# A gated mix of two attentions on one core: small vector work moved to GpSimd and ScalarE, and more score tasks and all projection jobs run before the attention loop

## The chip, the core and the metric

The kernel runs on one core of a Trainium2 chip. Its engines work side by side, each with a queue of its own in program order: TensorE (PE, with its weight loads as PEld), VectorE (DVE), ScalarE (ACT), GpSimd (POOL), and SyncE (SP), which issues most DMA transfers. The metric is the device time of one execution in microseconds; the median over several executions counts.

## The reference

Two attentions over the same input `x` (2048 × 512, 32 heads of 16) are mixed by a gate per row. A is causal within four segments of 512 rows, with a linear memory carried from segment to segment; B is full attention over all 2048 rows.

```python
def _A_ref(x, wq, wk, wv, wo, beta):            # H = 32; Dh = 16; N = 4 segments; L = 512
    ...
    phi = lambda t: jnp.where(t > 0, t + 1.0, jnp.exp(t))
    for s in range(N):
        qs, ks, vs = q[:, :, s], k[:, :, s], v[:, :, s]
        p = _softmax(jnp.einsum("bhqd,bhkd->bhqk", qs, ks) * scale + mask, axis=-1)
        a_dot = jnp.einsum("bhqk,bhkd->bhqd", p, vs)
        pq = phi(qs)
        num = jnp.einsum("bhld,bhde->bhle", pq, M)
        den = jnp.einsum("bhld,bhd->bhl", pq, z)[..., None] + 1e-6
        outs.append(g * num / den + (1.0 - g) * a_dot)
        pk = phi(ks)
        M = M + jnp.einsum("bhld,bhle->bhde", pk, vs)
        z = z + jnp.einsum("bhld->bhd", pk)
    return o @ wo
def _B_ref(x, wqkv, wo):
    ...
    p = _softmax(jnp.einsum("bhqd,bhkd->bhqk", q, k) * (Dh ** -0.5), axis=-1)
    o = jnp.einsum("bhqk,bhkd->bhqd", p, v)
    return o.transpose(0, 2, 1, 3).reshape(B, S, D) @ wo

g = _sigmoid((x * gate_w).sum(-1, keepdims=True))
return g * a + (1 - g) * b
```

## The kernel before

The work falls into two stages.

**The projection stage** computes V, Q and K of both attentions. Operands are split in a high and a low part, so that one job is three products: 12 matmuls into one PSUM bank (`v_job`, `qk_job`), then a rounding on ACT (line 348) and the remainder on DVE (line 349), and a store to DRAM by SP. After V of A and the first group of B, a loop over 16 blocks (`blk`) takes the Q and K of A, block by block of 128 columns by 512 rows, with the memory's updates between. Into its gaps two kinds of work are put: **fill jobs**, the 40 remaining jobs of B, in the order of the list `fill`, as many by the end of each block as `CUM` says; and **score tasks**, by `spill()`, two at a time whenever `quota` has grown to 2. 38 of these tasks (`first`) belong to the first units of both attentions, and the first `EARLY` tasks of unit 33 (`early`) come behind them. Four fill jobs are left over for slot 0.

**The attention loop** has 32 **slots**. Slot `k` handles unit `32 + k` of B and unit `k` of A; a unit is four heads by 512 query rows. In a slot PE makes 32 steps of B and 5 of A. A step (`t_group`) makes two score blocks, transposed so that keys lie on partitions, into two of three PSUM banks (line 635); ACT takes their exponentials into SBUF (line 641); for A, POOL zeroes what the causal mask excludes (line 644); and PE multiplies with V (`pv`, line 657), two steps later, into one bank, `PVB`, that all of it shares. `fin_copy` copies that bank out when a unit is complete: for B at the slot's end on ACT (line 666), for A at the start of the next slot on DVE (line 664).

The softmax's row maxima have to be known ahead. So the scores of unit `33 + k` of B and of `k + 1` of A are computed once more in slots before, in **score tasks** (`s_b`, line 572; `s_a`, line 550), 32 and 6 per slot, each with one maximum on DVE over 128 × 1024 (lines 574, 558, 560). Two PSUM buffers, `SBK`, hold them. `m_chain(k + 1)` gathers the maxima in step pair 10 of a slot (line 583), scales them and splits them in two fp16 parts (lines 597 to 599 on DVE, or 592 to 595 on POOL), and `m_rows` transposes them on PE and sends them into rows of the query tile, where the score matmul subtracts them.

`beside(k, it)` places the rest by step pair `it`: `fin_load` reads a finished unit back in another layout; `fin_rec` takes reciprocals of the denominators on DVE and multiplies them by the gates (line 687 or 689 on DVE; 684, 685, 689 on POOL); `fin_bc` spreads them over 64 partitions by DMA into `d`; `fin_norm` multiplies (line 701, POOL), every second slot. The output weights are read in slots 1 to 4 by `load_wo`, which also splits them (lines 713 and 714, POOL). From slot 9 on, the output projection (`out_rows`) is part of the slots.

The order on every engine is the order in which the program issues instructions; nothing reorders it, apart from the semaphores' waits.

Of the kernel before, what the change touches and what calls it, by code (L numbers as in the profile page):

```python
# [28 lines left out]
FAR = 2.0 ** 15  # L29
TOP = 2.0  # L30
WIDE = 2.0 ** 13
EARLY = 6
S_FIRST = 10
S_LAST = 10
OMI = 14
SPILLS = 64


@with_exitstack
def gated_mix_kernel(ctx, tc, xt, wq, wk, wv, wo, beta, wqkv, wob, gate_w, out):  # L40
    nc = tc.nc
# [536 lines left out]
    def m_chain(k):  # L578
        mx = pair_max(k)
        if k == 1:  # L580
            nc.vector.memset(mx[:, 0], 0.0)
        if k < 32:
            nc.vector.tensor_reduce(mx[:, 1], MXB.pop(32 + k).rearrange("q j p i c -> q (j p) i c"), axis=AX.X,
                                    op=OP.max)
        else:
            nc.vector.memset(mx[:, 1], 0.0)
        del MX[k]
        mx = mx.rearrange("q u h i -> q (u h i)")
        m8 = M8[k] = W.tile([128, 2, 32], FT, name="m8")
        hi = W.tile([128, 32], HF, name="mhi")  # L590
        if 8 <= k < 32:
            nc.gpsimd.tensor_scalar(mx, mx, -1.0 / AUX, None, op0=OP.mult)
            nc.gpsimd.tensor_copy(hi, mx)
            nc.gpsimd.tensor_copy(m8[:, 0], hi)
            nc.gpsimd.tensor_tensor(m8[:, 1], mx, hi, op=OP.subtract)
        else:
            nc.vector.tensor_scalar(hi, mx, -1.0 / AUX, None, op0=OP.mult)
            nc.vector.tensor_copy(m8[:, 0], hi)
            nc.vector.scalar_tensor_tensor(m8[:, 1], mx, -1.0 / AUX, hi, op0=OP.mult, op1=OP.subtract)
# [16 lines left out]
    AT = {}  # L616
# [43 lines left out]
    def fin_copy(u):  # L660

        ps = W.tile([128, C], FT, name="pvs", bufs=1)
        if u < 31:
            nc.vector.tensor_copy(ps, PVB)
        else:
            nc.scalar.activation(ps, PVB, AF.Copy)  # L666
        AT["pd", u] = D.tile([4, 32, C], FT, name=f"pd{u}")
        nc.sync.dma_start(AT["pd", u].rearrange("h r t -> (h r) t"), ps)
# [9 lines left out]
    def fin_rec(u):  # L678
        kd, qd, c = UN[u]
        r = AT.pop(("r", u))  # L680
        nc.vector.reciprocal(r, r)  # L681
        early = u % 32 < 7 or u in (31, 63)
        if kd == "A" and not early:
            nc.gpsimd.tensor_scalar(r, r, nq[:, qd:qd + 1], None, op0=OP.mult)
            nc.gpsimd.tensor_tensor(r, r, grow[:, 0, c], op=OP.mult)
        elif kd == "A":
            nc.vector.scalar_tensor_tensor(r, r, nq[:, qd:qd + 1], grow[:, 0, c], op0=OP.mult, op1=OP.mult)
        else:
            (nc.vector if early else nc.gpsimd).tensor_tensor(r, r, grow[:, 1, c], op=OP.mult)  # L689
        AT["rd", u] = D.tile([128, E], FT, name=f"rd{u}")  # L690
        nc.sync.dma_start(AT["rd", u], r)
# [16 lines left out]

    def load_wo(g):
        for a, w in enumerate((wo, wob)):  # L710
            raw = AT["o"][1][:, g, a]
            nc.sync.dma_start(raw, w[g * 128:(g + 1) * 128, :])
            nc.gpsimd.tensor_copy(AT["wh"][:, g, a], raw)
            nc.gpsimd.tensor_tensor(AT["wl"][:, g, a], raw, AT["wh"][:, g, a], op=OP.subtract)

# [82 lines left out]
    ST_A = [(0, None), (2, 0), (2, 1), (3, 0), (3, 1), (1, None)]  # L798
# [113 lines left out]
    def spill():  # L912
        nonlocal quota
        quota += rate
        if quota >= 2:
            quota -= 2
            for _ in range(2):
                (first or early).pop(0)()

    S0 = [b[:, 0] for b in SBK]  # L920
    CUM = (2, 4, 6, 9, 11, 13, 16, 18, 20, 22, 24, 27, 29, 32, 34, 36)
    for blk in range(16):
        g, c = divmod(blk, 4)
        pg, pc = divmod(blk - 1, 4)
        if blk == 4:
            mode["misc"] = TB + [MB, PVB]
        rate = len(ST_A + ST_B) / SPILLS if 4 <= blk < 14 else 0
        if blk == 14:
            for p in range(2):
                set_aux(KB[1][:, p], 0, nc.sync)  # L930
            load_kb(1, 0)
        n = blk + 1 + (c == 2)
        if c < 3 and n < 16:
            load_vm(n // 4, n % 4)
        qk_job(0, "A", g, 0, c)
        if c == 3 and g < 3:
            split_w(0, "A", g + 1, (0,))
        spill()
        if blk == 0:
            do_beta()  # L940
        if blk == 2:
            load_kb(0)
# [24 lines left out]
        if blk == 15:  # L967
            m_rows(0)
        want = CUM[blk]
        mt = [[], [], []]  # L970
        if c > 0:
            mt[0] += [todo(mem_out, g, c)]
            mt[2] += [todo(mem_put, g, c)]
        if c < NC4 - 1:
            mt[1 + (c == 0)] += [todo(mem_tr, g, c)]
        for n in range(3):
            for f in mt[n]:
                f()
            if blk == 14 and n == 2:
                quota = EARLY  # L980
            if mt[n]:
                spill()
            if g < 3 and (c, n) == (1, 2):
                top(("A", g + 1))
            if g < 3 and (c, n) == (2, 0):
                w_rng("A", g + 1)
            if g < 3 and (c, n) == (2, 2):
                w_esc("A", g + 1)
            if blk == 14:
                load_kb(1, 1 + n)  # L990
            if nf == 35:
                mode["misc"] = [MB, PVB, TB[1]]
            if nf < want:
                fill[nf]()
                spill()
                if nf in (15, 20):
                    load_w("B", 2 + nf // 20)
                if nf in (15, 20, 26):
                    split_w(2 if nf == 20 else 1, "B", nf // 5 - 2)
                for f, at in ((w_abs, (11, 17, 22)), (lambda *a: top(a), (12, 18, 23)), (w_rng, (13, 19, 24)),  # L1000
                              (w_esc, (14, 21, 25))):
                    if nf in at:
                        f("B", at.index(nf) + 1)
                nf += 1
        if blk == 13:
            for f in first:
                f()
            first, quota = [], 0
        if 0 < c < NC4 - 1:
            mem_upd(g, c)  # L1010
        if blk == 14:
            spill()
        if blk == 15:
            for f in early:
                f()
        if nf >= 16 and "vb" not in AT:
            AT["vb"] = 1
            load_vb(0)
# [42 lines left out]
    def extras(k):  # L1061

        pre, post = {}, {}
        if not k:
            for n in range(4):
                pre[2 * n] = [fill[n - 4]]
        post[2 * S_LAST + 4] = [todo(m_rows, k + 1)]
        for n, at in [(k - 9, 1)] + [(23, 2 * OMI)] * (k == 31):
            if n >= 0:
                rows = (n // 8, n // 2 % 4, n % 2)  # L1070
                pre[at] = [todo(out_rows, *rows, plan.pop((k, at))) if k < 31 else todo(out_mm, *rows)]
        return pre, post
# [41 lines left out]
    for k in range(31):  # L1114
        if k:
            spread([todo(s_b, 33 + k, *t) for t in (sorted(ST_B, key=lambda t: t[2]) if k == 1 else ST_B)],
                   [(k - 1, n) for n in range(2 * S_FIRST, 2 * NT)] + [(k, n) for n in range(2 * S_LAST)])
        else:
            spread(st33[EARLY:], sorted([(0, n) for n in range(2 * S_LAST)] + [(0, 2 * n) for n in range(4)]))
        for n, t in enumerate(ST_A):  # L1120
            plan.setdefault((k, 2 * NT + n - (n > 2)), []).append(todo(s_a, k + 1, *t))

    ex = [extras(k) for k in range(32)]
    for k in range(32):
        ua, ub = k, 32 + k
        banks = T3 + [b[:, 0] for b in SBK] * (k == 31)
        for n in range(NG):
# [27 lines left out]
            if it == 9:  # L1155
                if k % 2 == 0 and k < 30:
                    load_vb(k // 2 + 1)
                if 1 <= k <= 4:
                    load_wo(k - 1)
    pv(31, 2)  # L1160
    fin_copy(31)
    fin_bc(63)
# [52 lines left out]
```

## Time and profile before

| | |
|---|---|
| median of 3 runs | 1825.24 us (1824.66 to 1825.6) |
| the profiled execution | 1825.88 us, of which 1824.2 are the span of the profile |
| busy: PE, DVE, ACT, POOL | 98%, 87%, 80%, 19% of the span |
| projection stage | up to 324.86 us |
| slot 0 | 324.86 us to about 389.6 us |
| slots 1 to 8, copy to copy of `fin_copy` | 45.90, 45.07, 45.47, 44.81, 44.80, 44.80, 44.28, 43.66 us |
| slots 9 to 12 | 45.73, 45.66, 45.80, 45.66 us |
| granted clock of PE | 0.996 over the span |

A line of a timeline has start, duration, engine, line of the kernel, operation, what it writes from what it reads, shapes, and in brackets the idle time of the engine ahead of it with what ended that. Matmuls overlap, so a busy PE isn't PE at its peak. The granted clock is the share of full clock that the throttle allowed PE. The shares of busy time are means over stages with different limits; a stage is read by itself.

### The profile page before, as it was taken

What the parts mean: (1) busy time and instruction counts of PE and PEld (TensorE: products, weight loads), DVE (VectorE), ACT (ScalarE), POOL (GpSimd) and SP (SyncE); (2) the same over time, 40 slices, a digit from 0 to 9 for tenths busy, and PEclk for the clock granted to TensorE, in tenths of its full rate; (3) what the DMA queues carried; (4) which work ended last, traced back from release to release, by engine and by line L of the source; (5) the groups of instructions that cost most, each with busy time, mean ns of one, the idle gap of its engine ahead of it and who ended that gap; (6) DMA issues with size and microseconds to landing.
All of it is one profiled execution on the core that took longest, in us unless ns stands there. A gap on an engine that the chain in (4) does not pass through costs nothing.

```text
span 1824.2 us, 44323 instructions
## 1 busy us (share of the span) xinstructions
PE 1786.8 (98%) x17781; PEld 645.1 (35%) x17781; DVE 1590.9 (87%) x1787; ACT 1459.3 (80%) x2741; POOL 339.5 (19%) x691
## 2 busy tenths in 40 slices
PE   8999999999999999999999999999999999999998
PEld 6554445222222222333333333333333333333325
DVE  7745786699999999999999999999999999999932
ACT  4454444588989999989898989898989898989894
POOL 4400000001212111112121222122212221222122
PEclk9999999999999999999999999999999999999999
DMA  5654534322323232223232323232323232323111
GB/s 196 152 153 134 159 104 115 75 81 73 93 74 93 64 85 70 77 65 88 65 87 67 86 70 82 71 88 69 85 69 86 68 86 68 86 66 87 46 38 62
DMA packets 162482, 158.92 MB, mean 87 GB/s; under 512 B 40140, under 2 KB 126620, under 8 KB 162276
## 3 DMA queue, kind: packets, MB, share of 16 engines
q1 hardware_dynamic: 158692, 149.29, 29.5%
q0 software_dynamic: 3296, 6.27, 1.8%
q8 instruction: 140, 2.29, 0.5%
q14 instruction: 66, 0.54, 0.1%
q10 hardware_dynamic: 288, 0.52, 0.1%
HBM read 103.38 MB, written 50.86 MB: 85 GB/s over the span
## 4 chain that ended last, share of the span: by engine, by line
PE 78%; DVE 14%; ACT 4%; issue 2%; DMA 1%; POOL 0%; SPq 0%; ACTq 0%; DVEq 0%; POOLq 0%
PE pvb L657 28%; DVE mxb L574 12%; PE tb L635 12%; PE sbk L572 9%; PE mb L635 6%; PE tb L332 3%; ACT raw L641 3%; PE tb L742 2%; PE mb L332 2%; PE sbk L550 2%; PE tb L302 2%; PE sbk L302 2%; PE pvb L332 2%; PE mb L742 1%; PE sbk L332 1%
## 5 line engine op out<-in xcount | busy, mean ns | idle before, releaser
L574 DVE TENSOR_REDUCE mxb<-sbk 128x2 f32<-128x1024 f32 x1024 | 1172.5, 1212 | 21.7 <-PE sbk L572 11.1
L641 ACT ACTIVATE raw<-tb 128x512 f32<-128x512 f32 x1555 | 884.0, 600 | 61.1 <-PE tb L635 25.1
L657 PE MATMUL pvb<-raw,vb 128*17 128x256 f32 (+1 forms) x8072 | 644.4, 388 | 0.0
L572 PE MATMUL sbk<-kb,qb 64*128 64x512 f16 x2048 | 552.7, 378 | 8.4 <-DVE mxb L574 7.3
L641 ACT ACTIVATE raw<-mb 128x512 f32<-128x512 f32 x782 | 469.1, 600 | 33.7 <-PE mb L635 16.7
L635 PE MATMUL tb<-qb,kb 64*128 64x512 f16 x1342 | 467.9, 380 | 2.4 <-ACT raw L641 1.3
L635 PEld LDWEIGHTS <-kb 64*128 64x128 f16 x2048 | 143.5, 93 | 414.1 <-issue 408.8
L657 PEld LDWEIGHTS pvb<-raw,vb 128*17 128x17 f32 x8072 | 137.8, 95 | 402.9 <-issue 393.5
L635 PE MATMUL mb<-qb,kb 64*128 64x512 f16 x679 | 258.4, 381 | 0.0
L644 POOL TENSOR_SCALAR_AFFINE_SELECT raw<-raw 128x256 f32<-128x256 f32 (+1 forms) x320 | 115.4, 361 | 324.4 <-ACT raw L641 316.0
L572 PEld LDWEIGHTS <-qb 64*128 64x128 f16 x2048 | 137.4, 93 | 44.3 <-issue 33.7
L558 DVE TENSOR_REDUCE mx<-sbk 128x2 f32<-128x1024 f32 (+1 forms) x128 | 133.9, 1088 | 6.9 <-PE sbk L554 5.7
L657 PE MATMUL pvb<-raw,va 128*17 128x256 f32 (+2 forms) x1280 | 103.2, 383 | 3.7 <-ACT pvs L666 0.9
L701 POOL TENSOR_TENSOR o<-o,d 128x512 f32<-128x512 f32 x31 | 39.5, 1273 | 217.6 <-DMA d<-rd 156.6
L560 DVE TENSOR_REDUCE mx<-sbk 128x4 f32<-128x512 f32 x64 | 60.6, 947 | 12.5 <-PE sbk L554 12.5
L550 PE MATMUL sbk<-ka,qa 64*128 64x512 f16 (+3 forms) x512 | 70.7, 296 | 0.0
L635 PE MATMUL tb<-qa,ka 64*128 64x512 f16 (+3 forms) x339 | 61.8, 302 | 0.0
L347 DVE SCALAR_TENSOR_TENSOR phi<-phe,phi 128x512 f32<-128x512 f32 x24 | 16.6, 692 | 51.6 <-ACT phe L346 51.6
L689 POOL TENSOR_TENSOR rec<-rec,grow 128x16 f32<-128x16 f32 x24 | 5.3, 222 | 275.8 <-DVE rec L681 275.8
L554 PE MATMUL sbk<-cmask,crows 64*128 64x64 bf16 x1024 | 52.7, 189 | 0.0
L332 PEld LDWEIGHTS <-ws 128*128 128x128 f16 x384 | 37.1, 98 | 43.5 <-issue 2.9
L554 PEld LDWEIGHTS <-crows 64*128 64x128 bf16 x1024 | 46.4, 94 | 13.9
(358 smaller groups left out, 1621.8 us busy)
## 6 DMA issues: line engine op xcount, KB each, us to landing
vb<-vdB SPq DMA_DIRECT2D x16, 1088.0 KB
pd<-pvs SPq DMA_DIRECT2D x64, 256.0 KB
kb<-dB SPq DMA_DIRECT2D x60, 256.0 KB
dB<-st SPq DMA_DIRECT2D x64, 128.0 KB
dA<-st SPq DMA_DIRECT2D x64, 128.0 KB
o<-pd SPq DMA_DIRECT2D x64, 128.0 KB
d<-rd SPq DMA_DIRECT2D x63, 128.0 KB
kb<-dB SPq DMA_DIRECT2D x60, 128.0 KB
```

The lines of the kernel that those rows point to most:

```text
L302: nc.tensor.matmul(b, x[:, n % 4, tl * 128:(tl + 1) * 128], (WVA if kd == "A" else WV)[wi][:, n % 4, :], start=n == 0, stop=n == 11)
L332: nc.tensor.matmul(b, WS[ws][w][wi][:, k, :], (XH, XL)[xi][c][:, k, :], start=n == 0, stop=n == 11)
L550: nc.tensor.matmul(b[:, j, c0:c0 + n], q_of(u)[r, p, i * 128:(i + 1) * 128], k_of(u, p)[r, :n], start=True, stop=False)
L554: nc.tensor.matmul(b[:, j, c0 + n - 128 + w.start:c0 + n - 128 + w.stop], crows[r, n2 - 1], cmask[r, n2 - 1, w], start=False, stop=n2 == 2)
L558: nc.vector.tensor_reduce(m[:, :, p, i], b[:, :, :n], axis=AX.X, op=OP.max)
L560: nc.vector.tensor_reduce(m[:, :, :, i], b.rearrange("q j (p k) -> q j p k", p=2)[:, :, :, :n], axis=AX.X, op=OP.max)
L572: nc.tensor.matmul(b[:, j], q_of(u)[r, p, i * 128:(i + 1) * 128], k_of(u, p)[r, kc * C:(kc + 1) * C], start=True, stop=True)
L574: nc.vector.tensor_reduce(MXB[u][:, :, p, i, kc], b, axis=AX.X, op=OP.max)
L635: nc.tensor.matmul(bs[j][:, c0:c0 + w], k_of(u, h // 2)[r, 128 * it:128 * it + 128], q_of(u)[r, h // 2, q0:], start=True, stop=True)
L641: nc.scalar.activation(pt, bs[j], AF.Exp, scale=AT["esc", kd, qd // 2])
L644: nc.gpsimd.affine_select(out=m, in_=m, pattern=[[1, 128]] if n < 2 else [[0, 2], [1, 128]], compare_op=OP.is_ge, fill=0.0, base=0, channe ...
L657: nc.tensor.matmul(PVB[32 * h:32 * h + E + 1, q0 + lo:q0 + hi], vt[:, it, 4 * q + h, :], pt[:, lo:hi], start=it == 0 and lo == 0, stop=it ...
```

## The change

Four pieces of work change engine or place.

1. `m_chain` splits the maxima on POOL for `k` from 2 on (from 8 before): that is done in slots 1 to 6 in addition. `fin_rec` multiplies the gates on POOL for all units but 0, 31, 32 and 63 (before, the units 0 to 6 and 32 to 38 had DVE).
2. `fin_copy` of A's units 0 to 7, at the starts of slots 1 to 8, moves from DVE to ACT.
3. `load_wo` only loads; `split_wo`, new, splits the output weights in step pair 14 of slots 1 to 4, and not in step pair 9.
4. `EARLY` goes from 6 to 14, `spill` starts at block 3 with 0.62 of a task per call (block 4, 0.59 before), and `CUM` ends at 40: all fill jobs and 14 tasks of unit 33 run in the projection stage; slot 0 has no fill job and 8 score tasks fewer. Unit 33's keys are loaded whole in block 7.

```diff
-EARLY = 6
+EARLY = 14
-SPILLS = 64
+RATE = 0.62
...
-        if 8 <= k < 32:
+        if 2 <= k < 32:
             nc.gpsimd.tensor_scalar(mx, mx, -1.0 / AUX, None, op0=OP.mult)
...
     def fin_copy(u):
-        if u < 31:
+        if 8 <= u < 31:
             nc.vector.tensor_copy(ps, PVB)
         else:
             nc.scalar.activation(ps, PVB, AF.Copy)
...
     def fin_rec(u):
-        early = u % 32 < 7 or u in (31, 63)
+        early = u % 32 < 1 or u in (31, 63)
...
     def load_wo(g):
         for a, w in enumerate((wo, wob)):
+            nc.sync.dma_start(AT["o"][1][:, g, a], w[g * 128:(g + 1) * 128, :])
+
+    def split_wo(g):
+        for a in range(2):
             raw = AT["o"][1][:, g, a]
-            nc.sync.dma_start(raw, w[g * 128:(g + 1) * 128, :])
             nc.gpsimd.tensor_copy(AT["wh"][:, g, a], raw)
             nc.gpsimd.tensor_tensor(AT["wl"][:, g, a], raw, AT["wh"][:, g, a], op=OP.subtract)
...
-    CUM = (2, 4, 6, 9, 11, 13, 16, 18, 20, 22, 24, 27, 29, 32, 34, 36)
+    CUM = (2, 5, 7, 10, 12, 15, 17, 20, 22, 25, 27, 30, 32, 35, 37, 40)
...
-        rate = len(ST_A + ST_B) / SPILLS if 4 <= blk < 14 else 0
-        if blk == 14:
+        rate = RATE if blk > 2 else 0
+        if blk == 7:
             for p in range(2):
                 set_aux(KB[1][:, p], 0, nc.sync)
-            load_kb(1, 0)
+            load_kb(1)
...
-            if blk == 14 and n == 2:
-                quota = EARLY
...
-            if nf == 35:
+            if nf == 39:
                 mode["misc"] = [MB, PVB, TB[1]]
...
-        if not k:
-            for n in range(4):
-                pre[2 * n] = [fill[n - 4]]
...
-            spread(st33[EARLY:], sorted([(0, n) for n in range(2 * S_LAST)] + [(0, 2 * n) for n in range(4)]))
+            spread(st33[EARLY:], [(0, n) for n in range(2 * S_LAST)])
...
                 if 1 <= k <= 4:
                     load_wo(k - 1)
+            if it == 14 and 1 <= k <= 4:
+                split_wo(k - 1)
```

What stands in POOL's queue in slot 2 before, between the masks of slot 1 and its own (the `wh` and `wl` rows are the weights' parts, `d1` and `d0` the spread denominators of B and A, `raw8` the exponentials that are masked):

```order
L701 TENSOR_TENSOR o0_2997<-o0_2997,d1_3002 128x512
L713 CAST wh_2999<-o1_2998 128x512
L714 TENSOR_TENSOR wl_3000<-o1_2998,wh_2999 128x512
...
L701 TENSOR_TENSOR o0_2997<-o0_2997,d0_3001 128x512
L644 AFFINE_SELECT raw8_86<-raw8_86 128x128 x4
L644 AFFINE_SELECT raw8_86<-raw8_86 128x2x128 x6
```

And now, in slot 2:

```order
L689 TENSOR_TENSOR rec_3911<-rec_3911,grow_82 128x16
L684 TENSOR_SCALAR rec_3987<-rec_3987,nq_85 128x16
L685 TENSOR_TENSOR rec_3987<-rec_3987,grow_82 128x16
L701 TENSOR_TENSOR o0_2991<-o0_2991,d1_2996 128x512
L592 TENSOR_SCALAR mx_3818<-mx_3818 128x32
...
L595 TENSOR_TENSOR m8_4211<-mx_3818,mhi_4212 128x32
L701 TENSOR_TENSOR o0_2991<-o0_2991,d0_2995 128x512
L716 CAST wh_2993<-o1_2992 128x512
L717 TENSOR_TENSOR wl_2994<-o1_2992,wh_2993 128x512
...
L644 AFFINE_SELECT raw8_86<-raw8_86 128x128 x4
L644 AFFINE_SELECT raw8_86<-raw8_86 128x2x128 x6
```

Gate products and the maxima's split are new to the queue, and the weights' split (twice cast and subtract) has moved from ahead of the second line-701 product to between it and the masks. Slot 4 has the same order; slots 1 and 3 have no line-701 product.

On ACT the end of the projection and the start of slot 0 stand so before (line 348 rounds a fill job, line 1106 loads the exponentials' scales into registers, line 641 is an exponential):

```order
L452 ACTIVATE om<-tb_135,gh 128x512
L1106 TENSOR_LOAD esc x8
L641 ACTIVATE raw_86<-tb_134 128x512
L641 ACTIVATE raw_86<-mb 128x512
L348 ACTIVATE st<-tb_135,xr 128x512
```

And now:

```order
L452 ACTIVATE om<-pvb,gh 128x512
L348 ACTIVATE st<-tb_135,xr 128x512
L1103 TENSOR_LOAD esc x8
L641 ACTIVATE raw_86<-tb_134 128x512
L641 ACTIVATE raw_86<-mb 128x512
L641 ACTIVATE raw_86<-tb_135 128x512
```

The last fill job's rounding has moved from behind the first two exponentials to ahead of the register loads, and no further one stands among the exponentials.

More of the change, by code (lines that the diff above doesn't have):

```diff
@@ L916, in spill @@
             quota -= 2
-            for _ in range(2):
-                (first or early).pop(0)()
+            for f in (first or early)[:2]:
+                f()
+            del (first or early)[:2]
     S0 = [b[:, 0] for b in SBK]
-    CUM = (2, 4, 6, 9, 11, 13, 16, 18, 20, 22, 24, 27, 29, 32, 34, 36)
+    CUM = (2, 5, 7, 10, 12, 15, 17, 20, 22, 25, 27, 30, 32, 35, 37, 40)
     for blk in range(16):
@@ L988, in gated_mix_kernel @@
                 w_esc("A", g + 1)
-            if blk == 14:
-                load_kb(1, 1 + n)
-            if nf == 35:
+            if nf == 39:
                 mode["misc"] = [MB, PVB, TB[1]]
```

## The prediction

> **What bounds the kernel now.** I read first the busy time by stage, cut at each copy of the P·V accumulator (line 664), since that copy is made once per slot. Columns: window, length, busy of PE, PEld, DVE, ACT, POOL, granted clock, DMA.
>
> ```profile
> 324.86:391.35 66.49, 61.28 (x562) 18.61 (x562) 54.45 (x56) 45.98 (x85) 3.61 (x10) 0.95 0.28 78
> 391.35:437.25 45.90, 44.45 (x493) 12.99 (x492) 45.17 (x49) 40.67 (x77) 7.31 (x14) 1.00 0.28 77
> 572.60:617.40 44.80, 44.25 (x493) 12.96 (x492) 44.12 (x49) 40.80 (x77) 3.61 (x10) 1.00 0.24 63
> 662.20:706.48 44.28, 44.05 (x493) 12.97 (x492) 43.66 (x46) 40.70 (x77) 4.55 (x14) 1.00 0.23 63
> 706.48:750.14 43.66, 43.45 (x492) 12.90 (x492) 43.12 (x43) 41.29 (x78) 8.93 (x20) 1.00 0.33 88
> 750.14:795.87 45.73, 45.56 (x518) 14.68 (x520) 43.90 (x45) 40.66 (x78) 6.58 (x18) 1.00 0.23 59
> ```
>
> The first row is slot 0 from its first line-635 matmul, and runs 1.8 us into slot 1. The others are slots 1, 5, 7, 8 and 9. In slots 1 to 7 DVE is filled to 0.7 us of the slot, and the slot shortens whenever DVE loses work: 44.80 to 44.28 where the maxima's split goes to POOL, to 43.66 where the gate products follow. So VectorE paces slots 1 to 8. From slot 9 on, with the output projection, DVE idles 1.83 us and PE paces; those slots are untouched by the change.
>
> The timeline of DVE in slot 1, and of PE, POOL and DVE in slots 2 and 8, show what the moved work costs where it is:
>
> ```profile
> 391.35 0.68 DVE L664 COPY pvs<-pvb 128x512 f32<-128x512 f32 x1
> 391.94 12.52 DVE L574 TENSOR_REDUCE mxb<-sbk 128x2 f32<-128x1024 f32 x11
> 415.64 0.61 POOL L713 CAST wh<-o 128x512 fp32r<-128x512 f32 x1 [25.94 <-DVE mxb L574]
> 416.74 0.91 DVE L597 TENSOR_SCALAR mhi<-mx 128x32 f16<-128x32 f32 x1
> ...
> 462.64 0.18 DVE L597 TENSOR_SCALAR mhi<-mx 128x32 f16<-128x32 f32 x1
> 463.05 11.40 DVE L574 TENSOR_REDUCE mxb<-sbk 128x2 f32<-128x1024 f32 x10
> 463.85 0.61 POOL L713 CAST wh<-o 128x512 fp32r<-128x512 f32 x1 [6.91 <-DMA o<-in_A_wo_dram]
> 465.60 0.39 PE L635 MATMUL mb<-qb,kb 64*128 64x512 f16 x1
> 466.45 1.27 POOL L714 TENSOR_TENSOR wl<-o,wh 128x512 fp32r<-128x512 f32 x1
> 472.04 1.27 POOL L701 TENSOR_TENSOR o<-o,d 128x512 f32<-128x512 f32 x1 [4.33 <-DMA d<-rd]
> 472.18 0.39 PE L635 MATMUL mb<-qb,kb 64*128 64x512 f16 x1
> 473.32 0.39 PE L635 MATMUL tb<-qa,ka 64*128 64x512 f16 x1
> 474.60 0.29 POOL L644 TENSOR_SCALAR_AFFINE_SELECT raw<-raw 128x128 f32<-128x128 f32 x1 [1.28 <-ACT raw L641]
> 476.34 0.29 POOL L644 TENSOR_SCALAR_AFFINE_SELECT raw<-raw 128x128 f32<-128x128 f32 x1 [0.20 <-ACT raw L641]
> 476.91 0.62 PE L657 MATMUL pvb<-raw,va 128*17 128x256 f32 x8
> 480.54 0.39 PE L635 MATMUL mb<-qb,kb 64*128 64x512 f16 x1
> ...
> 731.33 0.29 POOL L592 TENSOR_SCALAR mx<-mx 128x32 f32<-128x32 f32 x1 [5.12 <-DVE mx L583]
> 732.13 0.24 POOL L595 TENSOR_TENSOR m<-mx,mhi 128x32 f32<-128x32 f32 x1
> ```
>
> DVE's maximum over one score task recurs every 1.14 us (11.40 for 10). PE, where it doesn't wait, makes a step in 1.10 us (465.60 to 472.18, six steps) and the five steps of attention A in 7.2 (473.32 to 480.54). A slot therefore needs 32 × 1.10 + 7.2 + 0.3 for the rows of maxima = 42.7 us of PE. That floor is 1 us under slot 8.
>
> **The cost, part by part. Slots 1 to 8.** Their sum, copy to copy, is 750.14 − 391.35 = 358.8 us.
> - The copy goes to ACT in slots 1 to 8 (units 0 to 7). DVE gets its next maximum 0.59 us earlier each time (391.35 to 391.94). ACT has 41.3 of 43.66 us filled in slot 8, and the copy is about 0.6 there too. It stands in ACT's queue ahead of the exponentials of the second group, whose bank PE wants for the third group, and so makes PE some 0.5 later there; but DVE, a whole maximum in arrears, takes that up, so I count it as hidden. If it isn't, it costs up to 0.6 × 8 = 4.8; it can't gain beyond DVE's 0.59.
> - Splitting the maxima on POOL in slots 1 to 6, and the gate products in slots 2 to 7, brings them to what slots 7 and 8 show. On POOL the split ends at 732.37, 1.04 us after its start, and slot 8 hides that. Slot 1 keeps its products on DVE: 0.5 more there.
> - The first step of the maxima's split takes DVE 0.91 us in slot 1, where the weight split runs beside it, against 0.18 in slot 2. Moved apart, that goes too; it is part of slot 1's 45.90.
>
> So the slots go to 43.66 − 0.6 = 43.06, just over PE's floor: 8 × 43.06 + 0.5 = 345.0.
> - Against it stands the weight split's new place. In slots 1 and 3 the queue of POOL is empty behind the maxima, and nothing waits. In slots 2 and 4 the split now stands behind line 701's second product, which waits for its denominators until 472.04, and ahead of the causal masks of line 644. The split takes 3.9 us (463.85 to 467.72), so the first mask starts at 472.04 + 1.4 + 3.9 = 477.3, not 474.60. The four masks then run back to back in 1.4 and end at 478.7, not 476.63. PE's P·V at 476.91 starts 0.3 behind the last mask already, so PE waits 2 us more, and in-order behind it wait the remaining groups and their score tasks. Cost 2 × 2.0 = 4.1. The lower end is 0, if the denominators land 2.7 us earlier; the upper end is the split's whole 3.9 in both slots, 7.8.
>
> Slots 1 to 8: 349.1, a gain of 9.7 us.
>
> **Projection and slot 0.** Rows of the chain, and PE at the start of slot 0:
>
> ```profile
> 264.07 5.18 PE tb L332 x24
> 306.94 0.61 PE L572 MATMUL sbk<-kb,qb 64*128 64x512 f16 x4
> 307.48 0.73 PE L473 MATMUL tb<-vm,pk 128*128 128x136 f32 x4
> L1106 ACTq TENSOR_LOAD <-esc x8: 272/332/1269, 325.0 to 329.0; - x8
> 324.86 0.39 PE L635 MATMUL tb<-qb,kb 64*128 64x512 f16 x1
> 329.33 0.60 ACT L641 ACTIVATE raw<-tb 128x512 f32<-128x512 f32 x1 [3.49 <-PE tb L332]
> 329.98 0.37 PE L635 MATMUL tb<-qb,kb 64*128 64x512 f16 x1 [1.34 <-ACT raw L641]
> ```
>
> Four fill jobs (12 matmuls, 2.6 us) and eight score tasks (0.27 each: two take 307.48 − 306.94) enter the projection: 10.4 + 2.2 = 12.6 us of PE. Their DVE work, some 12 us, lies beside it: of the 213 us before slot 0, DVE is idle in 76. PE's waits for the rounding of a projection on DVE (line 349), behind a pair of maxima, I leave as they are:
>
> ```profile
> PE tb L302 <- DVE st L349: 1.8, 2, 1.1
> PE tb L332 <- DVE st L349: 1.4, 2, 1.0
> PE mb L332 <- DVE st L349: 1.0, 1, 1.0
> 112.00:324.86 212.86, 206.75 (x1135) 106.41 (x1135) 136.42 (x248) 92.78 (x182) 15.89 (x26) 1.00 0.48 136
> ```
>
> They sum to 4.2 us (columns: total, times, longest; the last row is the stage's busy time); I allow ±3 for the new places. Slot 0 then starts at 324.9 + 12.6 = 337.5. Unit 33's keys, loaded whole in block 7 and not in pieces from block 14, and the fills' last stores, which leave SP's queue ahead of slot 0, cost nothing: SP isn't in the chain there, and unit 33's tasks still come last of all; were the keys late, PE's score tasks would wait for them one by one.
>
> Slot 0 itself loses the fills and the DVE excess. PE needs 42.7, less the last P·V of a slot before (0.6) and two score tasks (0.5): 41.6. To this comes the start. ACT loads eight scale registers from 325.0 on, and its first exponential comes 4.5 us after PE's first score group. PE gets that bank back 5.1 us after the first matmul (329.98). The new order wants it for the second half of the second group, which a running slot reaches after one step and a matmul, some 1.3 us: 3.8 us, which a fill job filled before and nothing fills now. And the clock:
>
> ```profile
> 307.99:311.40 3.41, 2.08 (x14) 1.09 (x14) 3.41 (x5) 0.00 (x0) 0.45 (x1) 1.00 0.49 142
> 328.47:331.88 3.41, 1.08 (x7) 0.36 (x8) 0.85 (x2) 2.55 (x5) 0.00 (x0) 0.98 0.18 65
> 331.88:338.40 6.52, 6.39 (x17) 1.84 (x17) 3.35 (x3) 1.29 (x3) 0.00 (x0) 0.50 0.16 43
> ```
>
> After 3.4 us in which PE was busy for 1.1, the granted clock was 0.50 for 6.5 us; after 2.1 busy it stayed full. The new start leaves PE about 1.1 us busy in 4.5, so I take the same 6.5 us at half clock: 3.0 lost. The Trainium skill, "TensorE: Matmul & The Clock Gate", HAM oscillation, asks only for no PE-idle gap over about 3.4 us. The trace differs: the clock fell with PE's longest single gap before it at 1.34.
>
> Slot 0 to the same mark: 41.6 + 3.8 + 3.0 + 1.8 = 50.2, against 66.5. Projection and slot 0 together: 12.6 − 16.3 = −3.7.
>
> **Sum.** −9.7 − 3.7 = −13.4. The profiled execution took 1825.88 us (span 1824.2 and 1.7 around it), 0.64 above the median of 1825.24; the sum gives 1812.5 for it and 1811.8 for the median.
>
> A rule that speaks against moving work to POOL: the Trainium skill, "GPSIMD Engine Reference", Engine selection, gives elementwise work to VectorE, GpSimd being about 2x slower for two-input operations. The trace agrees on the size (1.04 us for the split on POOL; 462.64 to 463.05, 0.41, on DVE). By that rule slots 1 to 6 would lose 0.6 each, 3.8 in all, where the rows of maxima are awaited; slot 8 is shorter with the split on POOL, so they aren't.
>
> **Rivals.**
> - *PE, not DVE, paces slot 8.* Then 43.66 is the end, and the copy gains nothing: 4.8 more, 1816.6. For it: PE busy is 43.45 of 43.66. Against: steps of 1.13 there beside 1.10 unhindered. 0.16.
> - *The clock stays up at slot 0.* For it: the second group's first half breaks PE's wait in two. Against: so did the matmuls at 329.98. 3.0 less: 1808.8. 0.14. By the Trainium skill's clock page, quoted above, this is the case that comes, as neither part of the wait reaches 3.4 us.
> - *The masks aren't held up*, since faster slots bring the denominators earlier in relation: 4.1 less, 1807.7. 0.12.
> - *The 2 us waits in slots 2 and 4 drop the clock as well*: 1.4 busy of 3.4 lies nearer to the 1.1 that dropped it than to the 2.1 that didn't, but only where the clock's window falls just there. 6.5 us at half clock twice: 6.5 more, 1818.3. 0.09.
> - *Slower: the projection stage turns bank-bound.* All 26 pairs of tasks now run there, two maxima each ahead of the rounding that frees PE's bank. Were every pair to stall PE by the longest seen, 1.07, that is 27.8 instead of 4.2, and 23.6 on the sum: 1835.4. It decides from (13.4 + 4.2) / 26 = 0.68 us a pair. Against: five such waits now, with 22 pairs. 0.04.
>
> **How the numbers follow.** The forecast, 1811.8, has 0.45. The range 1804 to 1819 takes in the two faster and the two slower rivals, with ±3 for the projection's waits at its lower end, and leaves out the bank-bound case and joint extremes. A change of 0.2% is 3.65 us, about what a measurement here can tell from none: faster means below 1821.6. All cases but the last are; with 1 in 50 for mishaps among them: 0.94 faster, 0.03 the same, 0.03 slower.
>
> **What would show it.** Slots 3, 5, 6, 7, 8 at 43.0 to 43.2 copy to copy and slot 1 at 43.6; DVE idle some 1 us in each; slots 2 and 4 at about 45, with PE waiting 2 us for line 644 behind the second weight split. First line-635 matmul near 337.5, slot 0 near 48 us with half clock in its first 10. Wrong if the slots stay at 43.6 or above, or if PE's waits for line 349 in the projection exceed 9 us.

## The result, and the profile after

The changed kernel took 1817.0 us (median of 5 runs, 1816.1 to 1818.0) beside 1825.3 us of the kernel before on the same chip: a ratio of 0.9948, 95% interval 0.9935 to 0.9962. The forecast was 1811.8, its range 1804 to 1819. The profiled execution took 1818.03 us (span 1816.3), 7.9 less than that of before; the sum of the prediction had said 13.4 less. So the sign and most of the gain came, and 5.5 us of it didn't.

Busy time by stage, in the columns used before (window, length, PE, PEld, DVE, ACT, POOL, granted clock, DMA): the projection from 112 us on, slot 0 from its first line-635 matmul to the copy, then slots 1, 2, 5, 8 and 9 from copy to copy. The copies of slots 0 to 7 are ACT's now (line 666), that of slot 8 is DVE's again.

```profile
112.00:341.39 229.39, 220.35 (x1199) 111.21 (x1197) 148.89 (x260) 96.27 (x186) 15.90 (x26) 1.00 0.49 131
341.39:391.60 50.21, 45.83 (x497) 12.39 (x497) 42.70 (x44) 41.71 (x79) 3.61 (x10) 0.93 0.30 82
391.60:435.47 43.87, 43.41 (x496) 12.45 (x493) 43.16 (x44) 40.61 (x78) 8.19 (x18) 1.00 0.29 77
435.47:480.12 44.65, 43.65 (x496) 12.76 (x493) 42.80 (x42) 40.57 (x78) 11.22 (x23) 1.00 0.39 101
568.22:611.47 43.25, 42.94 (x496) 12.48 (x493) 42.62 (x42) 40.57 (x79) 5.30 (x17) 1.00 0.21 57
697.97:741.61 43.64, 43.21 (x496) 12.55 (x494) 43.01 (x42) 41.70 (x80) 8.94 (x20) 1.00 0.33 89
741.61:787.35 45.74, 45.58 (x518) 14.68 (x520) 43.91 (x44) 40.66 (x78) 6.58 (x18) 1.00 0.21 57
```

Four readings, each against a row of before:
- Slots 1 to 8 last 741.61 − 391.60 = 350.0 us, not 358.8: −8.8. All but slots 2 and 4 (44.65, 44.67) lie at 43.25 to 43.9.
- Slot 0 starts at 341.39 and not at 324.86: +16.5. PE's busy time in the stage grew by 13.6 (206.75 to 220.35), its idle time from 6.1 to 9.0.
- Slot 0 to the copy takes 50.21 us, not 66.49: −16.3, with the clock at 0.93 on the mean.
- Slot 9 takes 45.74, as before (45.73). From there to the end 0.6 us of the gain is lost; the runs below differ by as much there, so no cause is given for it.

Slot 2, a timeline of PE and POOL (lines 716 and 717 are the weight split, 713 and 714 before):

```profile
468.99 1.28 POOL L701 TENSOR_TENSOR o<-o,d 128x512 f32<-128x512 f32 x1 [7.66 <-DMA d<-rd]
470.21 0.62 POOL L716 CAST wh<-o 128x512 fp32r<-128x512 f32 x1
472.82 1.26 POOL L717 TENSOR_TENSOR wl<-o,wh 128x512 fp32r<-128x512 f32 x1
474.04 1.75 POOL L644 TENSOR_SCALAR_AFFINE_SELECT raw<-raw 128x128 f32<-128x128 f32 x6
474.38 1.34 PE L657 MATMUL pvb<-raw,va 128*17 128x256 f32 x8 [0.78 <-POOL raw L644]
```

The six masks start at 474.04, the instant the split is done, and PE's P·V waits for the first of them. This is the hold-up that the prediction described, in its order and place.

The start of slot 0, a timeline of PE and ACT, then busy time around it:

```profile
341.39 0.39 PE L635 MATMUL tb<-qb,kb 64*128 64x512 f16 x1
343.02 0.37 PE L635 MATMUL tb<-qb,kb 64*128 64x512 f16 x1 [1.24 <-DVE st L349]
345.68 0.60 ACT L641 ACTIVATE raw<-tb 128x512 f32<-128x512 f32 x1 [3.49 <-DVE mxb L574]
346.32 0.58 PE L635 MATMUL tb<-qb,kb 64*128 64x512 f16 x1 [2.71 <-ACT raw L641]
```

```profile
341.00:344.40 3.40, 1.37 (x8) 0.22 (x6) 2.07 (x3) 0.69 (x1) 0.00 (x0) 1.00 0.54 182
344.40:347.80 3.40, 1.48 (x5) 0.23 (x4) 0.48 (x1) 2.12 (x5) 0.00 (x0) 0.67 0.51 140
347.80:351.20 3.40, 3.40 (x26) 0.57 (x24) 2.45 (x2) 2.00 (x4) 0.00 (x0) 0.50 0.36 100
```

ACT's first exponential comes 4.3 us after PE's first score matmul. PE is busy for 1.4 of 3.4 us, then the granted clock is at 0.50, and one line-635 matmul takes 0.58 instead of 0.39. DVE is named as the releaser of ACT, but the row of the scale loads tells what ACT did in the gap:

```profile
L1103 ACTq TENSOR_LOAD <-esc x8: 275/414/722, 341.5 to 344.9; - x8
```

PE's waits in the projection (total, times, longest):

```profile
PE pvb L381 <- DVE stat L364: 1.8, 1, 1.8
PE mb L381 <- DVE stat L364: 1.2, 1, 1.2
PE tb L332 <- DVE st L349: 1.1, 1, 1.1
PE pvb L302 <- DVE st L349: 1.0, 1, 1.0
PE tb L332 <- ACT wv L264: 1.0, 1, 1.0
PE pvb L434 <- DVE mst L478: 0.9, 1, 0.9
PE mb L332 <- DVE st L349: 0.8, 1, 0.8
PE tb L302 <- DVE st L349: 0.6, 1, 0.6
```

Line 349 costs 3.5 us in all, less than the 4.2 of before. What is new are the waits for line 364, DVE's maximum over a block of raw weights, which PE wants at line 381, and those for lines 264, 314 and 478. A timeline of DVE and PE around the first of line 381:

```profile
205.05 2.35 DVE L574 TENSOR_REDUCE mxb<-sbk 128x2 f32<-128x1024 f32 x2
207.32 0.74 DVE L349 SCALAR_TENSOR_TENSOR st<-tb,xr,st 128x512 f16<-128x512 f32 x1
207.98 1.27 DVE L364 TENSOR_REDUCE stat<-raw 128x1 f32<-128x512 f32 x2
209.39 0.38 PE L381 MATMUL mb<-ident,stat 128*2 128x128 f32 x2 [1.22 <-DVE stat L364]
```

A pair of maxima, a rounding and the statistic follow each other without a gap, and PE waits for the last.

### The profile page after: what moved, and what is told of

It is laid out like the page before. It is cut to its first block, busy times and chain, and to the rows that moved or that the text cites. A ratio compares the mean times of both kernels' runs of the same rounds, so it can differ in the third digit from the quotient of the medians.

```text
span 1816.3 us, 44320 instructions
## 1 busy us (share of the span) xinstructions
PE 1777.4 (98%) x17781; PEld 640.6 (35%) x17781; DVE 1581.3 (87%) x1749; ACT 1457.9 (80%) x2749; POOL 348.5 (19%) x733
## 4 chain that ended last, share of the span: by engine, by line
PE 84%; issue 5%; ACT 4%; DVE 3%; DMA 2%; POOL 1%; SPq 0%; ACTq 0%; POOLq 0%; DVEq 0%
PE pvb L657 34%; PE tb L635 14%; PE sbk L572 11%; PE mb L635 7%; ACT raw L641 3%; PE tb L332 3%; PE tb L745 2%; PE sbk L550 2%; DVE mxb L574 2%; PE sbk L302 1%; PE mb L745 1%; PE mb L332 1%; PE sbk L332 1%; PE tb L302 1%; PE pvb L332 1%
## 5 line engine op out<-in xcount | busy, mean ns | idle before, releaser
L572 PE MATMUL sbk<-kb,qb 64*128 64x512 f16 x2048 | 559.9, 378 | 0.9 <-ACT vb L314 0.5
L635 PEld LDWEIGHTS <-kb 64*128 64x128 f16 x2048 | 139.0, 93 | 418.1 <-issue 415.4
L572 PEld LDWEIGHTS <-qb 64*128 64x128 f16 x2048 | 132.9, 93 | 28.7 <-issue 19.4
L635 PE MATMUL tb<-qa,ka 64*128 64x384 f16 (+3 forms) x340 | 61.5, 302 | 0.0
```

The source lines that it names most:

```text
L572: nc.tensor.matmul(b[:, j], q_of(u)[r, p, i * 128:(i + 1) * 128], k_of(u, p)[r, kc * C:(kc + 1) * C], start=True, stop=True)
L635: nc.tensor.matmul(bs[j][:, c0:c0 + w], k_of(u, h // 2)[r, 128 * it:128 * it + 128], q_of(u)[r, h // 2, q0:], start=True, stop=True)
```

## The experiments

All are compared with the changed kernel's 1817.0 us and its trace, unless something else is said.

**1. The slots' parts alone.** The kernel before with the split and products on POOL, ACT's copy and the later weight split; projection as before. Against the changed kernel:

```diff
-EARLY = 14
-RATE = 0.62
+EARLY = 6
+SPILLS = 64
 ... (CUM, the place of unit 33's keys and slot 0's fill jobs as before)
```

> The kernel before with the change's parts for slots 1 to 8 alone (maxima split and gate products on GpSimd, copy of the accumulator on ScalarE in units 0 to 7, weight split at step 14); projection stage and fill jobs as before. Theory (slots and projection are separate accounts, and the slots hold the whole gain): the slots lose 8.8 us copy to copy, as in the changed kernel, slot 0 stays at 66.5 less the DVE copy at its end (0.6): 1825.3 - 8.8 = 1816.5, 1816 to 1817. Rival (the slots got short because the 8 score tasks and the fills had left slot 0, so that DVE came into slot 1 without arrears): slots 1 and 2 stay near 45, and the time is 1819 to 1822.

1817.2 us, ratio to before 0.9950 (0.9936 to 0.9964). Slot 0's copy is made at 391.97 (391.35 before), slot 9 starts at 742.27: 350.3 us for slots 1 to 8, −8.5. Slot 1 is as short as in the changed kernel:

```profile
391.97:435.87 43.90, 43.44 (x496) 12.45 (x493) 43.16 (x44) 40.81 (x79) 8.20 (x18) 1.00 0.29 77
```

So the slots' parts make the whole gain, and they do so without any help of the projection's.

**2. The projection's part alone.**

```diff
-        if 2 <= k < 32:
+        if 8 <= k < 32:
-        if 8 <= u < 31:
+        if u < 31:
-        early = u % 32 < 1 or u in (31, 63)
+        early = u % 32 < 7 or u in (31, 63)
 ... (weight split back in load_wo)
```

> The changed kernel with its parts for the slots undone, so that only the 8 score tasks and the 4 fill jobs have moved into the projection stage. By the prediction's sum -3.7 us: 1821.6. Theory after the changed kernel's trace (slot 0 starts 16.5 later, not 12.6, and is 16.3 shorter): the move is worth nothing, 1825.3 + 0.2 = 1825.5, and slots 1 to 8 stay at the 44.8 of before. Rival (the projection's longer waits come from the slots' parts somehow, for instance the copy): slot 0 starts at 337.5 and the time is 1821.6.

1827.1 us, ratio to before 1.0005 (0.9996 to 1.0014): no change. Projection, slot 0 and slot 1:

```profile
112.00:341.16 229.16, 220.43 (x1191) 110.77 (x1190) 148.32 (x258) 95.39 (x184) 15.89 (x26) 0.99 0.49 131
341.16:391.43 50.27, 45.92 (x498) 12.49 (x498) 42.99 (x44) 42.02 (x80) 3.61 (x10) 0.93 0.31 84
391.43:437.17 45.74, 44.26 (x493) 12.98 (x492) 45.06 (x48) 40.81 (x77) 7.30 (x14) 1.00 0.28 74
```

Slot 0 starts 16.3 us later than before and is 16.2 shorter; its copy stands at 391.43, where it was at 391.35. Slots 1 to 8 last 358.8 us, as before. The forecast's −3.7 for this part was wrong by all of it.

**3. The weight split ahead of the products.**

```diff
-            if it == 14 and 1 <= k <= 4:
+            if it == 11 and 1 <= k <= 4:
```

> The changed kernel with the weight split issued at step 11 of slots 1 to 4 and not at step 14, that is ahead of line 701's first product in GpSimd's queue. Theory (the split holds up the causal masks in slots 2 and 4, which stand behind it): those two slots fall from 44.65 to the 43.25 of slots 5 to 7, 2.8 us in all: 1817.0 - 2.8 = 1814.2. Rival (slots 2 and 4 are long because the weights' transfers or GpSimd's traffic beside DVE stretch PE's and DVE's work): they keep 44.65 and the time is 1817. A smaller rival: the product of line 701 comes after the split and its store late, which moves 1 us or more into the next slot.

1812.6 us, ratio to before 0.9930 (0.9916 to 0.9943). Slots 1 to 8 last 347.2 us: 2.8 less, as expected to the tenth. The median fell by 4.5, though the span of its profile fell by 2.5; the slots' own rows carry the verdict. Slots 2 and 4, then POOL in slot 2:

```profile
435.97:479.23 43.26, 42.94 (x496) 12.48 (x493) 42.63 (x42) 40.58 (x79) 11.55 (x23) 1.00 0.36 98
522.65:565.90 43.25, 42.77 (x494) 12.45 (x492) 42.46 (x42) 40.57 (x78) 11.55 (x23) 1.00 0.35 97
```

```profile
466.65 1.27 POOL L717 TENSOR_TENSOR wl<-o,wh 128x512 fp32r<-128x512 f32 x1
469.61 1.27 POOL L701 TENSOR_TENSOR o<-o,d 128x512 f32<-128x512 f32 x1 [1.68 <-DMA d<-rd]
471.98 0.29 POOL L644 TENSOR_SCALAR_AFFINE_SELECT raw<-raw 128x128 f32<-128x128 f32 x1 [1.10 <-ACT raw L641]
```

The split ends before the denominators land, and each mask waits for ACT alone. The traffic of the weights is the same and costs nothing.

**4. The scale registers loaded earlier.** Two per block in the last four blocks of the projection.

```diff
+        if blk > 11:
+            load_scales(blk - 12)
         qk_job(0, "A", g, 0, c)
 ...
-    for i, kd in enumerate("AB"):
-        for g in range(4):
-            AT["esc", kd, g] = nc.scalar.alloc_register(f"esc{kd}{g}")
-            nc.scalar.reg_load(AT["esc", kd, g], esc.bitcast(I32)[0:1, i, g:g + 1])
```

> The changed kernel with ScalarE's eight scale-register loads issued two at a time at the start of the last four blocks of the projection, not in one piece ahead of slot 0. Theory (the loads, 4.3 us from 272 ns to 1269 ns each, make ScalarE's first exponential late; PE waits 2.7 us for it and its clock then stands at 0.50 for 6.5 us): both go, slot 0 falls from 50.2 to 43.5 to 44.5, and the time is 1817.0 - 6 = 1811, 1810 to 1812. Rival 1 (the clock drops at the seam of the stages anyway, as PE still waits 1.2 us there for a rounding on DVE): only the wait goes, 1814.3. Rival 2 (each load stalls ScalarE as long in the projection, where its copies free PE's banks): the projection grows by up to 4 us and the gain is under 3. The Trainium skill, "TensorE: Matmul & The Clock Gate", HAM oscillation, has the clock stay up where no gap of PE is over about 3.4 us; by that rule there would be no clock term to win, here or in the changed kernel.

1812.8 us, ratio to before 0.9937 (0.9924 to 0.9951). Slot 0, and a stretch that had the clock at 0.67 in the changed kernel:

```profile
340.90:385.85 44.95, 43.24 (x497) 12.43 (x497) 42.34 (x44) 41.74 (x80) 3.61 (x10) 1.00 0.35 92
344.40:347.80 3.40, 3.40 (x41) 0.74 (x36) 3.40 (x4) 3.28 (x7) 0.00 (x0) 1.00 0.53 148
```

Slot 0 lost 5.3 us: 2.7 of wait for ACT, and 2.6 of PE's busy time (45.83 to 43.24), which was the half clock. PE's 1.24 us for line 349 stayed, and alone didn't lower the clock. So slot 0 ends 0.4 us above the expected range, and the time 0.8. The loads cost nothing in the projection, which is as long as before them.

**5. Score tasks one at a time.**

```diff
-        if quota >= 2:
-            quota -= 2
-            for f in (first or early)[:2]:
+        if quota >= 1:
+            quota -= 1
+            for f in (first or early)[:1]:
```

> The changed kernel with the score tasks of the projection stage issued one at a time as soon as the quota reaches one, not two at a time when it reaches two. Theory (a pair of maxima, 2.35 us, stands in VectorE's queue ahead of the roundings and statistics that free PE's banks, lines 349, 364, 478): the ten waits of PE in the projection, 9.0 us, halve, slot 0 starts 3 to 4.5 earlier than 341.4 to 342.5, and the time is 1817.0 - 3.5 = 1813.5. Rival 1 (the waits come from the transfers of unit 33's keys, which now run beside the same blocks): nothing changes, 1817. Rival 2 (one maximum ahead of twice as many roundings costs as much as two ahead of half): 1817 as well, but with more and shorter waits.

1824.2 us, 7 us slower than the changed kernel, which no theory had. Slot 0 starts at 345.91. PE's waits sum to much the same, but its score matmuls of line 572 in the projection do not (this kernel, then the changed one; length of the window, PE, PEld, clock, DMA):

```profile
112.00:345.91 233.91, 17.94 (x92) 4.50 (x92) 1.00 0.47 129
```

```profile
112.00:341.39 229.39, 14.37 (x92) 2.97 (x92) 1.00 0.49 131
```

The same 92 matmuls take 3.6 us more: in the timelines a task alone holds PE for 0.39 us, two together for 0.60. Of the 6.5 us by which the span is longer, 4.5 lie ahead of slot 0 and 1.2 in it, where PE waits 3.7 and not 2.7 us for ACT. The pairs are right, and what PE saves by them is more than what DVE's longer pieces cost it.

**6. Unit 33's keys later.**

```diff
-        if blk == 7:
+        if blk == 11:
             for p in range(2):
                 set_aux(KB[1][:, p], 0, nc.sync)
             load_kb(1)
```

> The changed kernel with unit 33's keys loaded in block 11 of the projection and not in block 7. Rival to the queue of VectorE (the keys' transfers delay other loads and stores, and these PE's waits): the waits around 205 to 243 us go, slot 0 starts 3 us earlier, 1814. Theory (the waits are VectorE's order alone): slot 0 starts at 341.4 to 342.5 as before and the time is 1817 within 1.

1816.7 us, no change that can be measured. Slot 0 starts at 340.9, and kernels with the projection stage of the changed one (itself and experiments 2, 3, 7 and 8) start it at 341.2 to 343.1. But one wait of PE is gone. It is that of line 332 for line 349 near 220 us: 1.05 in the changed kernel, and anything from none (experiment 4) to 2.2 in other runs with the keys in block 7. ACT and PE there, first in the run of experiment 9, which names the releaser, then in this one:

```profile
220.62 0.69 ACT L348 ACTIVATE st<-tb,xr 128x512 f16<-128x512 f32 x1 [9.29 <-DMA dA<-st]
222.15 1.02 PE L332 MATMUL tb<-xp,wv 128*128 128x512 f16 x4 [2.18 <-DVE st L349]
```

```profile
214.35 0.69 ACT L348 ACTIVATE st<-tb,xr 128x512 f16<-128x512 f32 x1 [2.55 <-PE tb L332]
220.37 1.90 PE L332 MATMUL tb<-xp,wv 128*128 128x512 f16 x8
```

With the keys in block 7, ACT stands 5.6 to 9.3 us for a buffer of `st` whose store hasn't landed, and DVE behind it. PE feels 0 to 2.2 us of that. With the keys in block 11, here and in experiment 12, this stop of ACT is gone. So both theories hold a part: this wait is the transfers', and the others stayed, as they would if they are DVE's order.

**7. Half of the maxima's columns** for units 34 to 40, to see what paces slots 5 to 7.

```diff
-        nc.vector.tensor_reduce(MXB[u][:, :, p, i, kc], b, axis=AX.X, op=OP.max)
+        nc.vector.tensor_reduce(MXB[u][:, :, p, i, kc], b[:, :, :C // 2] if 34 <= u < 41 else b, axis=AX.X, op=OP.max)
```

> The changed kernel with the maxima of units 34 to 40 (line 574, mostly slots 1 to 7) taken over half of the columns, which leaves half of that work out. It tells what paces slots 5 to 7 at 43.25 us, where the prediction had 43.06 and a floor of 42.7 for PE. If VectorE still paces them, they fall to 42.7 or below with about 13 us of VectorE gone. If PE paces them (its steps of 1.095 and a short wait for ScalarE behind the copy), they stay within 0.1 of 43.25, and no more work taken from VectorE can pay.

One execution; its slot 5:

```profile
564.84:607.34 42.50, 42.02 (x496) 11.64 (x493) 28.54 (x41) 40.27 (x78) 5.33 (x17) 1.00 0.21 57
```

With DVE filled to two thirds, the slot takes 42.5 us. So VectorE still paces the changed kernel's slots, though it idles 0.63 us in each, more than PE's 0.31. Where the idle time lies, around the copy at 611.47 that ends slot 5 of the changed kernel:

```profile
606.01 3.22 DVE L558 TENSOR_REDUCE mx<-sbk 128x2 f32<-128x768 f32 x3 [0.16 <-PE sbk L554]
610.71 3.49 DVE L574 TENSOR_REDUCE mxb<-sbk 128x2 f32<-128x1024 f32 x3 [0.35 <-PE mb L635]
612.62 0.37 PE L635 MATMUL tb<-qb,kb 64*128 64x512 f16 x1 [0.23 <-ACT raw L641]
```

DVE waits 0.16 and 0.35 us for PE ahead of the copy, and as much in slot 8 of before. Only the last 0.1 is new; it fits PE's wait of 0.23 for ACT behind the copy.

**8. ACT's copy in all slots.**

```diff
-        if 8 <= u < 31:
+        if u < 0:
             nc.vector.tensor_copy(ps, PVB)
```

> The changed kernel with the copy of the accumulator on ScalarE in all slots, from slot 9 on too. Theory (from slot 9 on PE paces, so an engine that has idle time gains nothing): slots 9 to 30 keep their lengths (45.7 in slot 9) within 0.1 and the time is 1817 within 1; what it may cost is a wait of PE of 0.2 behind ScalarE's queue per slot, 4.4 in all. Rival (the copy is worth 0.4 to 0.6 there as in slots 1 to 8): 22 x 0.4 to 0.6, 9 to 13 us less, 1804 to 1808.

1818.7 us (1816.0 to 1824.2), ratio to before 0.9967 (0.9957 to 0.9977), so nothing gained. Slot 9 takes 45.70, and DVE has 0.64 less in it than in the changed kernel:

```profile
742.71:788.41 45.70, 45.50 (x518) 14.62 (x516) 43.27 (x43) 41.06 (x80) 6.94 (x18) 1.00 0.22 59
```

From there to the end of the span it is 1075.1 us, and 1074.7 in the changed kernel. Where PE paces, the same edit that was worth 0.4 us a slot is worth nothing.

**9. Statistics ahead of the pair.**

```diff
                 fill[nf]()
-                spill()
 ...
                 nf += 1
+                spill()
```

> The changed kernel with the pair of score tasks that follows a fill job issued behind the weights' statistics of that job (lines 364, 381 and those after) and not ahead of them. Theory (in the projection PE waits at line 381 for VectorE's line 364, which stands behind a pair of maxima of 2.35 us): the two waits there, 3.0 us together in the changed kernel, fall to under 1, slot 0 starts 2 to 3 earlier, near 339, and the time is 1817.0 - 2.5 = 1814.5. Rival (VectorE is in arrears there by more than the pair, with the roundings of lines 347, 349 and 443 as well; the score tasks that covered part of the wait are then gone from ahead of it): the waits stay at 2.5 or more and the time is 1816 to 1818.

1817.5 us. The waits at line 381 stayed at 1.2 and 1.8, but the run doesn't decide: the edit moved one pair behind lines 417 and 418 only. The pairs ahead of line 364 are those after a memory job of the step, which it didn't touch.

**10. No pair just ahead of a statistic.** On top of the last edit:

```diff
-            if mt[n]:
+            if mt[n] and nf not in (11, 17, 22):
                 spill()
```

> The run before it moved only one pair of maxima, and not one of the two that stand ahead of a statistic PE waits for. Here the changed kernel gives up the pair after a memory job where a weights' statistic follows in the same step (fill jobs 11, 17 and 22), and issues the pair of that step behind the statistic. At both places line 364 then has no pair in VectorE's queue just ahead of it. Theory: the two waits at line 381, 1.2 and 1.8 us, go under 0.3 each and slot 0 starts 2 to 3 us earlier for it, 1814.5; other waits may come up where the pairs land. Rival (VectorE is in arrears by all that stands there, or the pairs make an equal wait at their next place, since the stage has 76 tasks to place): the sum of PE's waits in the projection stays within 1 us of the changed kernel's 9, 1816 to 1818.

1814.0 us, ratio to before 0.9947 (0.9933 to 0.9961). Slot 0 starts at 339.3 us, 2.1 earlier than in the changed kernel and 1.9 earlier than in any run with its projection stage, and its copy comes at 388.5, 3.1 earlier. The waits at line 381:

```profile
PE mb L381 <- DVE stat L364: 0.3, 1, 0.3
```

3.0 us have become 0.3, and the waits of the stage sum to some 7. A wait of 1.0 for the maxima (line 572) has come up for it at the seam. So the pair of maxima in DVE's queue is shown as the cause of these two waits; the 1 us above them came from slot 0, where PE waited 1.3 and not 2.7 for ACT.

**11. The two edits of 3 and 4 together.**

> The changed kernel with both edits that gained: weight split at step 11, scale registers loaded in the last four blocks of the projection. Theory (the two stand in different stages and add up: 2.8 us in slots 2 and 4, 5.3 in slot 0): 1817.0 - 8.1 = 1808.9, 1808 to 1810. Rival (a slot 0 that ends earlier meets the first weights' transfer and its denominators later in relation, so that slot 2 waits again): 1811.

1810.0 us, ratio to before 0.9915 (0.9901 to 0.9928). Slot 0 takes 44.94, slots 1 to 8 347.2: both gains are there in full. The projection of this execution was 1.3 us longer, half of it in the wait behind the keys (1.7 and not 1.05).

**12. Four edits: 3, 4, 6 and 10.**

> The changed kernel with the four edits together: weight split at step 11, scale registers loaded in the last four blocks of the projection, unit 33's keys loaded in block 11, and no pair of maxima just ahead of the weights' statistics. Theory (four places, four separate waits): -2.8 in slots 2 and 4, -5.3 in slot 0, -1.0 for the wait behind the keys, -2.0 in the projection for the pairs (the rest of that run's gain lay in the scale loads' wait, which is gone here anyway): 1817.0 - 11.1 = 1805.9, 1804.5 to 1807.5. Rival (waits shift to the next place when one goes, as the projection's sum of waits did in the run with single tasks): 1808 to 1810, no better than the two edits alone.

1807.5 us (1806.2 to 1807.6), ratio to before 0.9897 (0.9880 to 0.9913): the fastest of all, at the upper end of what was expected. Its span is 10.5 us under the changed kernel's: 7.9 up to the copy of slot 0, 2.7 in slots 1 to 8. The projection ends near 336.5 us, 4.9 earlier, but slot 0 then takes 47.2 and not 45. Of these 2.3 us, 0.8 are waits: PE now waits for the maxima of the pairs that had been put off. The other 1.5 are PE's busy time (44.73, and 43.24 in experiment 4), since the granted clock is at 0.50 for 3.4 us:

```profile
336.50:339.90 3.40, 1.38 (x9) 0.39 (x6) 3.01 (x4) 2.49 (x5) 0.00 (x0) 1.00 0.50 143
341.00:344.40 3.40, 3.40 (x28) 0.60 (x24) 2.65 (x4) 2.01 (x5) 0.00 (x0) 0.50 0.40 107
337.69 0.37 PE L635 MATMUL tb<-qb,kb 64*128 64x512 f16 x1 [0.80 <-DVE st L349]
338.82 0.39 PE L572 MATMUL sbk<-kb,qb 64*128 64x512 f16 x2 [0.76 <-DVE mxb L574]
```

So a part of the rival holds: some of that wait was only moved, and the half clock came back with it, though ACT's loads no longer stand there and no gap of PE is over 0.80 us.

## Why the prediction was right, and where its sum was off

**The copy.** "So the slots go to 43.06": they went to 43.25. The copy was worth 0.41 (slot 8 of before 43.66, slots 5 to 7 now 43.25) and not DVE's whole 0.59. DVE's busy time in a slot fell by 0.50 (43.12 to 42.62), and its idle time rose by 0.09, so "DVE idle some 1 us" didn't come either. The 0.09 fits PE's short wait for ACT behind the copy, which the prediction counted as hidden; no run takes that wait away by itself. Over eight slots 1.5 us. The first rival, that PE paces slot 8 and the copy gains nothing, named nearly the time that came (1816.6) for a reason that experiment 7 excludes: PE alone would go at 42.5.

**The masks.** Right in place, chain and slots, but 1.4 us a slot and not 2.0. The masks themselves were held up as forecast: the first starts 38.6 us into slot 2, and 36.0 in experiment 3, so 2.6 later (2.7 forecast). But the forecast let PE's P·V begin behind the last mask; it begins at 474.38, behind the first, and goes along with them (8 matmuls in 1.34 us, 0.62 before). Experiment 3 shows the cause by taking it away. The rival without hold-up falls; so does that of a clock drop there (1.00 in slots 2 and 4).

Slots 1 to 8 by these terms: 8 × 43.25, 0.6 for slot 1's products, 2 × 1.4 for the masks, 0.2 for slot 3 and 0.4 for DVE's copy at the end of slot 8, 350.0. (Where ACT makes that copy too, in experiment 8, slot 8 takes 43.30.) The forecast had 349.1.

**Slot 0.** 50.2 was forecast and 50.21 came: 3.9 of wait (3.8 forecast), 2.6 of half clock (3.0) and 43.7 without them (43.4), so the agreement to the tenth is luck. Experiment 4 shows that ACT's eight loads made 2.7 of the wait and the half clock. The other 1.24 us of wait, for DVE's line 349, isn't the loads': it stayed there, and the forecast had put all 3.8 to ACT. The rival "the clock stays up" falls. By the Trainium skill, "TensorE: Matmul & The Clock Gate", HAM oscillation, it should have stood, as no gap of PE reached 3.4 us: here the gaps were 1.24 and 2.71, with 0.6 us of matmuls between, and the clock went to 0.50. In experiment 12 it went to 0.50 with no gap over 0.80. The next section of the Trainium skill there, A second HAM failure mode, where frequent short idles of PE lower the clock, is nearer to these traces, but gives no number to forecast by.

**The projection: the step that failed.** "PE's waits [...] I leave as they are." All of PE's waits in the stage went from 6.1 to 9.0 us, just within the ±3 that the prediction allowed for line 349's, and PE's busy time grew by 13.6, not 12.6: the four fill jobs by the forecast's 10.4 (line 332: 130.3 to 140.7), line 572 by 2.7 instead of 2.2, and 0.5 spread over other lines. Together this is 3.9 us, the largest part of the 5.5. The prediction watched line 349, the largest releaser in the table of before, and that one became cheaper (4.2 to 3.5). The pairs now stood ahead of other short DVE work that PE wants, above all the weights' statistics; experiment 10 takes 2.7 us of that away by moving those pairs. And unit 33's keys, counted at nothing since SP isn't in the chain there, hold up stores that free `st`: 1.05 us of PE's wait here, 0 to 2.2 in other runs (experiment 6). So the move was worth 0 and not −3.7, as experiments 1 and 2 show from both sides.

**The slower rival** had its mechanism in part, pairs of maxima ahead of what PE waits for, but not at every pair: 9.0 us of waits and not 27.8.

**The rule on GpSimd** by which slots 1 to 6 would lose 0.6 each (the Trainium skill, "GPSIMD Engine Reference", Engine selection) did not bear here: the work is slower on POOL, and each of slots 1 to 6 got shorter.

## What to carry to other kernels

Work taken from an engine pays only where that engine paces: the same copy gave some 0.4 us a slot up to slot 8 and nothing from slot 9 on. The shares of idle time alone didn't tell who paces, for in slots 5 to 7 DVE idles more than PE; halving DVE's work did. When work moves into a stage, list everything short in the queue it joins, not only the wait that the profile already shows: the new waits came at lines that had none. And a burst of small set-up instructions at a seam can cost twice, once as a wait and once as a lowered clock; spread over the stage before, it cost nothing. The lowered clock can come from other waits too, as in experiment 12, so it has to be looked for after every change to the seam.

## What the runs showed of the hardware

- Two score tasks in a row, each of two 64-row matmuls, hold PE for 0.60 us; one alone holds it for 0.39. 46 tasks issued one at a time cost PE 3.6 us more than in pairs.
- Eight register loads of ACT, 275 to 722 ns each, held its first exponential for 3.5 us at the seam and cost nothing in the four blocks before.
- The clock was at 0.50 after 3.4 us with 1.4 of PE busy and gaps of 1.2 and 2.7; with the first gap alone (experiment 4, 2.1 busy) it stayed at 1.00. In experiment 12 it was at 0.50 for 3.4 us after 3.4 us with 1.4 busy and no gap over 0.80.
